# An attention scheduler that keeps two engines out of each other's way in its plan, and a new order

## The chip, the cores and the metric

One core of a Trainium2 chip runs the whole program. The time is in device microseconds for one execution. Engines: PE (matrix products), DVE, ACT and POOL (elementwise work), SP (issues most DMAs). Each engine takes its instructions from a queue of its own, in the order in which the program put them there; semaphores tie the queues together.

## The reference

Three layers in a row, in float32:

```python
q_rot, k_rot = rotate(q), rotate(k)              # 4 batches, 8 heads, 576 positions, 64 columns
attn = softmax(q_rot @ k_rot.T / sqrt(64))
x = (attn @ v).transpose(0, 2, 1, 3).reshape(2304, 512)
x = (sigmoid(x @ w_gate) * (x @ w_val)) @ w_out  # 512 -> 1536 -> 512
e = argmax(x @ w_gate2 + bias[modality])         # one of 8 experts for each token
out = prob[e] * (relu(x @ w1[e]) @ w2[e])        # 512 -> 1024 -> 512
```

## The kernel before

The three layers stand one behind the other: the attention (class `Attention`), the gated layer (`Gated`) and the experts (`Experts`). Products of float32 are made from two parts of a number, a high part (a cast) and a low part (the number less its high part), so nearly every tile gets a cast on ACT or POOL and a subtraction on DVE or POOL.

The attention works on 16 pairs of heads (p), each in 9 tiles of 128 query rows (T = 9 p + t). For a tile:

- PE makes the scores (`scores`, L183) into one of 2 PSUM tiles `s`;
- DVE takes them out, scaled, with the row minimum (`evac_scores`, L193), into one of 11 tiles `e`;
- ACT makes the exponentials with their sums (`exp`, L205);
- PE transposes them in four pieces (`transpose`, L237) into one of 3 PSUM tiles `pt`;
- ACT casts the high part `pth` (`pt_hi`, L267) and DVE subtracts for the low part `ptl` (`pt_lo`, L271).

When half a pair's tiles are there, PE multiplies by v (`value`, L284); ACT copies one half of the result (L292) and DVE adds (`value_add`, L301) into `xy`. Later the row sums, sent through DRAM as `rr`, normalise the pair's outputs (`normalise`, L231, on DVE or POOL).

The preparation of a pair runs one pair ahead. SP loads q and k with their half-swapped copies into `sa` (L328). For each half (q is 0, k is 1) POOL or DVE multiplies by the rotation table (`rope_op`, L162 for both products at once, 1152 columns; L164 for one) and adds (L160); then comes the cast (L152 on ACT, L154 on POOL) and the low part (L437: `sa<-sa` for q, `kl<-sa` for k, on DVE or POOL). SP then copies the parts to other partitions (L455). v gets a cast and a low part too (L349). The next load of a half waits until the low part of the same half is made. Pairs 0 and 1 go another way (`plan_direct`): the rotation is cut into pieces of columns (L164, L160), k-low is L383 and q-low L398. The conversion of the first gated weights (L654 to L681) fills gaps.

The order in every queue is made by `Plan` while the program is built. Each operation is added with its engine, an assumed cost, the operations it needs and a priority. `order` keeps a clock for each engine; it takes the engine that can start something first and, of what is ready there, the operation of the lowest priority number. An operation is done a latency `LAT` after its cost. Limits on buffers (`rings`) are counted too. Tables say who does what: `DIRECT` and `KLO` (pieces of pairs 0 and 1 on POOL), `LO`, `HI`, `VLO`, `VHI`, `ROPE`, `RM` (an engine for a pair's low part, cast, v, rotation, normalisation). `PR` and `OFF` move the priorities of kinds of operations against a tile's number.

The plan sets only the order in the queues. On the chip an instruction starts when its engine is free and its semaphores have come; the planned start times are not kept.

Below is what the change touches.

Of the kernel before, what the change touches and what calls it, by code (L numbers as in the profile page):

```python
# [31 lines left out]
class Plan:  # L32
# [4 lines left out]
    LAT = {"PE": 0.25, "SP": 0.65, "DMA": 2.0}  # L37

    def __init__(self, rings=(), free=()):
        self.ops = []  # L40
        self.free = dict(free)
        self.rings = dict(rings)
        self.takes = {}
        self.frees = {}

    def add(self, eng, cost, fn, deps, prio, ring=None):
# [5 lines left out]
    def order(self):  # L52
# [11 lines left out]

        def at(i):
            r = self.takes.get(i)
            if r and len(taken[r]) >= self.rings[r]:
                t = done[self.frees[taken[r][-self.rings[r]]]]
                return float("inf") if t is None else max(t, ready[i])
            return ready[i]  # L70
# [6 lines left out]
        while len(out) < n:  # L77
# [12 lines left out]
            free[e] = end  # L90
            self.start[i] = t
# [15 lines left out]
class Attention:  # L107
# [197 lines left out]
    def op(self, key, eng, cost, fn, deps=(), prio=0.0, ring=None):  # L305
# [5 lines left out]
        self.ids[key] = self.plan.add(eng, cost, fn, ds, prio, ring)  # L311
# [150 lines left out]
    DIRECT = ((0, 0, 0, 0), (0, 0, 1, 0), (0, 1, 0, 0), (0, 1, 0, 2), (1, 0, 0, 0), (1, 0, 0, 2), (1, 1, 0, 0), (1, 1, 0, 2),)  # L462
    NDIRECT = 2
    KLO = ((0, 0, 0), (0, 1, 1), (1, 0, 0),)
    LO = dict.fromkeys(((4, 0), (4, 1), (5, 0), (6, 0), (6, 1), (7, 1), (8, 0), (8, 1), (9, 1), (11, 1), (12, 0), (12, 1), (14, 1), (15, 0), (15, 1),), "POOL")
    VLO = dict.fromkeys((9, 14,), "DVE")
    ROPE = dict.fromkeys(((1, 0), (1, 1), (2, 0), (6, 0),), "DVE")
    PR = dict(ahead=-5.46, k=-139.78, split=-159.58, v=-65.53)
    RM = dict.fromkeys((0, 1, 2, 4, 5, 6, 7, 10, 12, 15,), "DVE")
    HI = dict.fromkeys(((2, 0), (2, 1), (3, 0), (5, 0), (6, 0), (6, 1), (7, 1), (8, 0), (9, 1), (10, 1), (11, 0), (12, 1), (13, 0), (14, 0), (14, 1), (15, 0),), "POOL")  # L470
    VHI = dict.fromkeys((1, 2, 4, 8, 9, 10,), "POOL")
    OFF = dict(table=0.16, xs=728.99, gv=822.87, post=977.12, rr=92.46, rm=165.62, s=-46.75, tsa=13.27, exp=86.93, eps=-141.16, rec=-185.35, norm=-135.21, tr=37.99, hi=46.49, lo=16.94, tr5=-62.52, val=70.55, vc=-103.28, va=-328.79)
# [138 lines left out]
class Gated:  # L611
# [202 lines left out]
    def opening(self):  # L814
# [10 lines left out]
        def op(key, eng, cost, fn, deps, prio, ring=None):  # L825
            ids[key] = plan.add(eng, cost, fn, [ids.get(d) for d in deps], prio, ring)
# [857 lines left out]
```

## Time and profile before

| | us |
|---|---|
| median of 3 runs | 1053.02 |
| lowest, highest run | 1049.65, 1053.76 |
| the profiled execution | 1049.16 |
| its span, first to last instruction | 1046.8 |
| PE busy in the span | 994.3 (95%) |
| DVE busy | 680.7 (65%) |
| ACT busy | 530.6 (51%) |
| POOL busy | 367.8 (35%) |

The shares of the whole span mix the three layers: the attention takes the first 320 us or so, the gated layer goes on to about 800 us, the experts take the rest. Which engine sets the pace has to be read for a stretch of time. Busy time is from start to end of an instruction as recorded, so an instruction that stands still half way counts as busy.

### The profile page before, as it was taken

Reading aid. Unit: us, or ns where it says so; the run is one execution under the profiler, and the core shown is the slowest. Engines: PE = TensorE matmul, PEld = TensorE weight load, DVE = VectorE, ACT = ScalarE, POOL = GpSimd, SP = SyncE. Lnnn points to the kernel's source line nnn. Section 1 sums busy time; section 2 is a strip of 40 time slices with the busy share of each in tenths; the row PEclk is TensorE's granted clock in tenths of the full one; section 3 lists DMA queues with packets and bytes.
Section 4 is the critical chain, followed back from the end, with each engine's and each line's share of the span. In section 5 each row is a group of like instructions: output and inputs, shape, how many; then the busy total and the mean of one; then the engine's idle time right before and its main releaser. Section 6 shows DMA issues by size and latency. Waiting matters only on the chain.

```text
span 1046.8 us, 16540 instructions
## 1 busy us (share of the span) xinstructions
PE 994.3 (95%) x6035; PEld 910.9 (87%) x6035; DVE 680.7 (65%) x1194; ACT 530.6 (51%) x1045; POOL 367.8 (35%) x279
## 2 busy tenths in 40 slices
PE   4989999989999999999999999999997999999996
PEld 2779898888998999999999999998975899999995
DVE  7999999999986756545535535522376755555651
ACT  5879898889886523212222212223331645555542
POOL 5578578677312422223223223311161012111111
PEclk9999999999999999999999999999998899999998
DMA  6568677767521311101101101000046877766650
GB/s 192 170 152 226 148 200 182 193 173 200 146 62 54 99 43 42 61 21 47 55 21 61 41 21 61 21 1 1 1 133 183 305 232 233 221 221 223 221 171 24
DMA packets 74136, 127.23 MB, mean 122 GB/s; under 512 B 14447, under 2 KB 37631, under 8 KB 74048
## 3 DMA queue, kind: packets, MB, share of 16 engines
q1 hardware_dynamic: 60128, 108.53, 35.7%
q0 software_dynamic: 3040, 9.70, 2.8%
q10 hardware_dynamic: 10880, 7.87, 2.4%
q8 instruction: 50, 0.82, 0.3%
q14 instruction: 38, 0.31, 0.1%
HBM read 95.65 MB, written 9.77 MB: 101 GB/s over the span
## 4 chain that ended last, share of the span: by engine, by line
PE 52%; issue 18%; DVE 16%; DMA 8%; POOL 3%; ACT 3%; SPq 0%; POOLq 0%; DVEq 0%; ACTq 0%
PE gv L721 28%; PE yo L787 13%; DMA out<-e_y,r_si 5%; DVE e L193 5%; DVE ptl L271 4%; PE pv L284 3%; PE s L183 3%; PE pt L237 2%; POOL e_xg L1452 1%; DVE xy L301 1%; ACT e L205 1%; PE s L721 1%; DMA sb<-sa 1%; PE r_pl L1221 1%; PE r_pt L1185 1%
## 5 line engine op out<-in xcount | busy, mean ns | idle before, releaser
L730 POOL TENSOR_TENSOR gl<-sg,gh 128x384 fp32r<-128x384 f32 x60 | 64.8, 1079 | 266.3 <-ACT gh L729 266.3
L728 DVE TENSOR_TENSOR sg<-gv,sg 128x384 f32<-128x384 f32 x70 | 39.0, 557 | 139.9 <-PE gv L721 119.9
L205 ACT ACTIVATE e<-e,st 128x576 f32<-128x576 f32 x144 | 112.3, 782 | 21.2 <-DVE e L193 20.5
L1445 DVE TENSOR_TENSOR e_w<-wr,e_w 128x1024 fp32r<-128x1024 f32 x80 | 96.0, 1223 | 28.4 <-ACT e_w L1444 28.1
L727 ACT ACTIVATE sg<-gv 128x384 f32<-128x384 f32 x70 | 34.4, 491 | 146.5 <-PE gv L721 146.3
L193 DVE TENSOR_SCALAR_CACHE_REDUCE e<-s 128x576 f32<-128x576 f32 x144 | 105.9, 744 | 1.6 <-PE s L183 0.9
L183 PE MATMUL s<-sb 128*128 128x288 f32 x320 | 78.8, 337 | 21.6 <-DVE sb L398 14.0
L271 DVE TENSOR_TENSOR ptl<-pt,pth 128x512 fp32r<-128x512 f32 x144 | 95.1, 679 | 1.5 <-ACT pth L267 0.4
L1444 ACT CAST e_w<-wr 128x1024 fp32r<-128x1024 f32 x80 | 81.5, 1048 | 23.1 <-DMA x_rows<-xy 20.6
L1500 PE MATMUL e_py<-e_w,e_hh 128*128 128x512 f32 x288 | 89.6, 392 | 0.0
L1515 POOL DMA_INDIRECT out<-e_y,r_si x19 | 19.6, 1030 | 187.7 <-ACT e_y L1514 177.5
L237 PE MATMUL pt<-cst,e 128*128 128x128 f32 x576 | 81.3, 279 | 3.0 <-DVE ptl L271 2.8
L267 ACT CAST pth<-pt 128x512 fp32r<-128x512 f32 x144 | 79.2, 587 | 7.7 <-PE pt L237 6.7
L1482 PE MATMUL e_ph<-e_xh,e_w 128*128 128x256 f32 x576 | 82.0, 286 | 0.7 <-ACT e_xh L1465 0.7
L162 POOL TENSOR_TENSOR sa<-sa,rope 128x1152 f32<-128x1152 f32 x26 | 69.5, 2674 | 37.1 <-DMA sa<-in_qk 29.6
L729 ACT CAST gh<-sg 128x384 fp32r<-128x384 f32 x60 | 30.8, 514 | 99.6 <-DVE sg L728 99.6
L183 PEld LDWEIGHTS s<-sb 128*128 128x128 f32 x320 | 51.3, 200 | 32.9 <-DVE sb L398 14.6
L284 PE MATMUL pv<-pth,vv 128*128 128x256 f32 (+1 forms) x256 | 73.9, 311 | 5.8 <-DVE xy L301 4.1
L721 PE MATMUL gv<-xe,wb 128*128 128x384 f32 x384 | 78.9, 338 | 0.0
L1482 PEld LDWEIGHTS e_ph<-e_xh,e_w 128*128 128x128 f32 x576 | 75.9, 195 | 1.7 <-ACT e_xh L1465 1.1
L721 PE MATMUL gv<-xh,wb 128*128 128x384 f32 x288 | 74.1, 338 | 0.0
L237 PEld LDWEIGHTS pt<-cst,e 128*128 128x128 f32 x576 | 67.9, 143 | 7.0 <-DVE ptl L271 2.8
(246 smaller groups left out, 2493.3 us busy)
## 6 DMA issues: line engine op xcount, KB each, us to landing
wr<-in_w SPq DMA_DIRECT2D x74, 512.0 KB
sa<-in_qk SPq DMA_DIRECT2D x30, 576.0 KB
sb<-sa SPq DMA_DIRECT2D x84, 144.0 KB
wraw<-in_wg SPq DMA_DIRECT2D x12, 512.0 KB
wraw<-in_wv SPq DMA_DIRECT2D x12, 512.0 KB
wraw<-in_wo SPq DMA_DIRECT2D x12, 512.0 KB
vraw<-in_v SPq DMA_DIRECT2D x16, 320.0 KB
x_rows<-xy ACTq DMA_DIRECT2D x18, 256.0 KB
```

The source lines that it names most:

```text
L183: nc.tensor.matmul(ps[:, u, 0:SH], a, m[:, SH * u:SH * u + SH], start=n == 0, stop=n == len(mm) - 1)
L193: self.nc.vector.tensor_scalar(out=e, in0=ps[:, :, 0:SH], scalar1=-0.125, scalar2=3.0e38, op0=ALU.mult, op1=ALU.min, accum_out=st[:, 0])
L205: nc.scalar.activation(out=e, in_=e, func=AF.Exp, bias=st[:, 0], scale=-1.0, accum_out=st[:, 1])
L237: nc.tensor.transpose(pt[:, c], e[:, 128 * c:128 * c + 128], self.ident)
L271: self.nc.vector.tensor_tensor(out=lo, in0=src, in1=f32(hi), op=ALU.subtract)
L284: nc.tensor.matmul(ps[:, 0:w], a, m, start=n == 0, stop=n == len(mm) - 1)
L721: self.nc.tensor.matmul(p[:, 0:U], a[:, wc], b[:, c], start=c == 0 and n == 0, stop=c == KC - 1 and n == 2)
L787: nc.tensor.matmul(ps, a, b, start=n == 0, stop=n == 3 * len(GROUPS[grp]) - 1)
L1444: nc.scalar.copy(out=hi, in_=raw)
L1445: nc.vector.tensor_tensor(out=lo, in0=raw, in1=f32(hi), op=ALU.subtract)
L1482: nc.tensor.matmul(ps[:, k], a[:, fs], b[:, c], start=n == 0, stop=n == 3 * KC - 1)
L1500: nc.tensor.matmul(ps, a[:, f, hs], b, start=n == 0, stop=n == 23)
```

## The change

The planner gets a set `shared`: all operations of POOL, and those of DVE that read two operands from SBUF or belong to the conversion of weights (normalisation, low parts of v, q and k, rotation, parts of x, the last step of the gate). It keeps one clock `port` for the set: a shared operation cannot start before the last shared one has ended, on whichever of the two engines that was. The assumed DMA latency goes from 2.0 to 2.2. All tables of shares and priorities get new numbers. No instruction is added to the program, and none gets another shape except the pieces of pairs 0 and 1 that change engine.

```diff
-    LAT = {"PE": 0.25, "SP": 0.65, "DMA": 2.0}
+    LAT = {"PE": 0.25, "SP": 0.65, "DMA": 2.2}
...
-    def add(self, eng, cost, fn, deps, prio, ring=None):
+        self.shared = set()
+
+    def add(self, eng, cost, fn, deps, prio, ring=None, shared=False):
+        if shared and eng == "DVE" or eng == "POOL":
+            self.shared.add(len(self.ops))
...
+        port = 0.0
+
         def at(i):
             r = self.takes.get(i)
+            t0 = max(ready[i], port) if i in self.shared else ready[i]
             if r and len(taken[r]) >= self.rings[r]:
                 t = done[self.frees[taken[r][-self.rings[r]]]]
-                return float("inf") if t is None else max(t, ready[i])
-            return ready[i]
+                return float("inf") if t is None else max(t, t0)
+            return t0
...
             free[e] = end
+            if i in self.shared:
+                port = end
...
-        self.ids[key] = self.plan.add(eng, cost, fn, ds, prio, ring)
+        shared = key[0] in ("rm", "vlo", "rope", "rot", "klo", "qlo", "xs", "cv") or key[0] == "lo" and len(key) == 3
+        self.ids[key] = self.plan.add(eng, cost, fn, ds, prio, ring, shared or key[0] == "post" and key[2] == 3)
...
-    KLO = ((0, 0, 0), (0, 1, 1), (1, 0, 0),)
+    KLO = ((0, 1, 1), (1, 0, 0), (1, 1, 0),)
...
-    PR = dict(ahead=-5.46, k=-139.78, split=-159.58, v=-65.53)
+    PR = dict(ahead=-305.08, k=-8.83, split=-1473.89, v=-316.64)
...
-            ids[key] = plan.add(eng, cost, fn, [ids.get(d) for d in deps], prio, ring)
+            ids[key] = plan.add(eng, cost, fn, [ids.get(d) for d in deps], prio, ring, key[0] in ("xl", "cv"))
```

What the other tables say, counted: low parts of q and k on POOL, 20 in place of 15 of 28 (both of a pair in nine pairs, in place of five); low parts of v on DVE, 6 in place of 2 of 16; normalisations on DVE, 7 in place of 10 of 16; casts of q and k on POOL, 13 in place of 16; casts of v on POOL, 7 in place of 6; pieces of the first two rotations on POOL, 5 in place of 8. The whole rotations (L162) on DVE stay two. In the changed file the lines stand 8 further down, from the middle of the class on 9.

Two places of the order. First POOL at the start, around the k-low of pair 1 (`kl_100`). Before:

```order
L164 TENSOR_TENSOR sa<-sa,rope 128x576
L383 TENSOR_TENSOR kl_100<-sa,sb 64x576
L160 TENSOR_TENSOR sa<-sa 128x576
L154 TENSOR_SCALAR vv_98<-vraw 128x10x64
L681 TENSOR_TENSOR wr<-wt,wr 128x512
L349 TENSOR_TENSOR vv_98<-vraw,vv_98 128x10x64
L162 TENSOR_TENSOR sa<-sa,rope 128x1152
```

and with the change:

```order
L172 TENSOR_TENSOR sa<-sa,rope 128x576
L168 TENSOR_TENSOR sa<-sa 128x576
L690 TENSOR_TENSOR wr<-wt,wr 128x512
L392 TENSOR_TENSOR kl_100<-sa,sb 64x576 x2
L170 TENSOR_TENSOR sa<-sa,rope 128x1152
L168 TENSOR_TENSOR sa<-sa 128x576
```

The addition for q that stood behind the k-low and both operations on v have left this piece of POOL's queue; the second k-low, which was DVE's, has come in, right ahead of the first whole rotation of pair 2.

Second DVE in pair 5 (numbers tell tiles apart: an `e` is a tile's scores as evacuated, a `pt` its transposed exponentials). Before, from the evacuation of `e_1430` to its low part, which is `pt_1515`:

```order
L193 TENSOR_SCALAR e_1430,st_1331<-s_1377 128x576
L271 TENSOR_TENSOR ptl_94<-pt_1399,pth_93 128x4x128
L193 TENSOR_SCALAR e_1447,st_1331<-s_1408 128x576
L193 TENSOR_SCALAR e_1457,st_1331<-s_1441 128x576
L301 TENSOR_TENSOR xy_73<-pv_1415,xv_105 64x256
L271 TENSOR_TENSOR ptl_94<-pt_1433,pth_93 128x4x128
...
L193 TENSOR_SCALAR e_1535,st_1331<-s_1503 128x576
L271 TENSOR_TENSOR ptl_94<-pt_1515,pth_93 128x4x128
```

and with the change, from `e_1403` to its low part, which is `pt_1435`:

```order
L201 TENSOR_SCALAR e_1403,st_1404<-s_1388 128x576
L201 TENSOR_SCALAR e_1418,st_1404<-s_1396 128x576
L446 TENSOR_TENSOR kl_0_99<-sa_103 128x576
L446 TENSOR_TENSOR sa_103<-sa_103 128x576
L309 TENSOR_TENSOR xy_73<-pv_1406,xv_105 64x320
L279 TENSOR_TENSOR ptl_94<-pt_1435,pth_93 128x4x128
L279 TENSOR_TENSOR ptl_94<-pt_1443,pth_93 128x4x128
```

Before, the low part stands 13 rows behind the evacuation (the fence leaves out six), which is the median of all 144 tiles; with the change five rows, where the median is 9. The preparation's low parts now stand ahead of the exponentials' when both can be had.

## Rows read from the trace of the kernel before

**Rows 1.** Busy time by stretch (us), instructions; PE, PEld, DVE, ACT, POOL; clock, DMA.

```profile
110.00:140.00 30.00, 28.32 (x221) 27.15 (x220) 29.67 (x68) 26.53 (x64) 23.20 (x14) 1.00 0.75 187
230.00:260.00 30.00, 28.83 (x223) 27.55 (x222) 28.86 (x65) 27.35 (x65) 22.17 (x15) 1.00 0.68 180
420.00:500.00 80.00, 80.00 (x426) 75.30 (x425) 38.94 (x58) 19.91 (x38) 21.55 (x19) 1.00 0.15 47
```

**Rows 2.** Groups of DVE, 0 to 322 us: busy us, mean ns, idle us before.

```profile
L193 DVE TENSOR_SCALAR_CACHE_REDUCE e<-s 128x576 f32<-128x576 f32 x144 | 105.9, 744 | 1.6 <-PE s L183 0.9
...
L231 DVE TENSOR_TENSOR xy<-xy,rr 128x576 f32<-128x576 f32 x10 | 13.2, 1317 | 1.6 <-DMA rr<-recip_rows 1.5
...
L437 DVE TENSOR_TENSOR sa<-sa 128x576 fp32r<-128x576 f32 x8 | 8.7, 1088 | 0.0
...
L383 DVE TENSOR_TENSOR kl<-sa,sb 64x576 fp32r<-64x576 f32 x1 | 4.7, 4685 | 0.0
L663 DVE TENSOR_SCALAR wt<-wt 128x512 int32<-128x512 int32 x3 | 4.6, 1544 | 0.0
...
L672 DVE SCALAR_TENSOR_TENSOR wt<-wraw,wt 128x512 int32<-128x512 int32 x3 | 3.5, 1180 | 0.0
...
L658 DVE TENSOR_SCALAR wt<-wt 128x512 f32<-128x512 f32 x3 | 3.1, 1037 | 0.0
```

**Rows 3.** Single lines on DVE: ns shortest/median/longest, first and last start, forms.

```profile
L437 DVE TENSOR_TENSOR sa<-sa x8: 736/1046/1593, 47.0 to 252.4; 128x576 fp32r<-128x576 f32 x8
...
L663 DVE TENSOR_SCALAR wt<-wt x36: 411/427/2675, 19.2 to 669.7; 128x512 int32<-128x512 int32 x36
...
L672 DVE SCALAR_TENSOR_TENSOR wt<-wraw,wt x36: 681/692/1668, 21.6 to 675.5; 128x512 int32<-128x512 int32 x36
...
L271 DVE TENSOR_TENSOR ptl<-pt,pth x144: 623/681/693, 25.0 to 310.2; 128x512 fp32r<-128x512 f32 x144
...
L164 DVE TENSOR_TENSOR sa<-sa,rope x7: 446/529/1757, 5.6 to 23.7; 128x288 f32<-128x288 f32 x3, 128x576 f32<-128x576 f32 x2, 128x256 f32<-128x256 f32 x1, 128x320 f32<-128x320 f32 x1
```

**Rows 4.** Timeline from 26 us: start us, us, engine, line; POOL without a break.

```profile
26.26 1.40 POOL L160 TENSOR_TENSOR sa<-sa 128x576 f32<-128x576 f32 x1
...
27.02 4.68 DVE L383 TENSOR_TENSOR kl<-sa,sb 64x576 fp32r<-64x576 f32 x1
...
29.55 1.53 POOL L349 TENSOR_TENSOR vv<-vraw,vv 128x640 fp32r<-128x640 f32 x1
```

**Rows 5.** Timeline around 209 us: DVE beside POOL.

```profile
208.79 2.67 POOL L162 TENSOR_TENSOR sa<-sa,rope 128x1152 f32<-128x1152 f32 x1 [1.59 <-DMA sa<-in_qk]
...
208.99 3.09 DVE L231 TENSOR_TENSOR xy<-xy,rr 128x576 f32<-128x576 f32 x1
```

**Rows 6.** Groups of POOL, 0 to 322 us.

```profile
L162 POOL TENSOR_TENSOR sa<-sa,rope 128x1152 f32<-128x1152 f32 x26 | 69.5, 2674 | 37.1 <-DMA sa<-in_qk 29.6 <-DVE rt L218 2.4 <-DVE e L193 2.0
L160 POOL TENSOR_TENSOR sa<-sa 128x576 f32<-128x576 f32 x28 | 42.4, 1522 | 3.1 <-DVE sa L164 2.3
...
L437 POOL TENSOR_TENSOR kl<-sa 128x576 fp32r<-128x576 f32 x9 | 14.1, 1561 | 10.4 <-PE s L183 10.2
...
L231 POOL TENSOR_TENSOR xy<-xy,rr 128x576 f32<-128x576 f32 x6 | 8.6, 1431 | 24.6 <-DMA rr<-recip_rows 12.8 <-DVE ptl L271 6.9 <-DVE xy L301 4.8
```

**Rows 7.** Waits, 0 to 322 us: us in total, times, longest us.

```profile
POOL sa L162 <- DMA sa<-in_qk: 29.6, 15, 5.3
```

**Rows 8.** Groups of ACT, 0 to 322 us.

```profile
L205 ACT ACTIVATE e<-e,st 128x576 f32<-128x576 f32 x144 | 112.3, 782 | 21.2 <-DVE e L193 20.5
L267 ACT CAST pth<-pt 128x512 fp32r<-128x512 f32 x144 | 79.2, 587 | 7.7 <-PE pt L237 6.7
```

**Rows 9.** Timeline of DVE: the first evacuation of pair 1, and of pair 15.

```profile
37.66 0.75 DVE L193 TENSOR_SCALAR_CACHE_REDUCE e<-s 128x576 f32<-128x576 f32 x1
...
285.81 0.74 DVE L193 TENSOR_SCALAR_CACHE_REDUCE e<-s 128x576 f32<-128x576 f32 x1
```

More of the change, by code (lines that the diff above doesn't have):

```diff
@@ L460, in plan_prep @@
         self.ready[p] = [[("dup", p, 0), ("dup", p, 1), ("lo", p, 1)]] * TPP
-    DIRECT = ((0, 0, 0, 0), (0, 0, 1, 0), (0, 1, 0, 0), (0, 1, 0, 2), (1, 0, 0, 0), (1, 0, 0, 2), (1, 1, 0, 0), (1, 1, 0, 2),)
+    DIRECT = ((0, 0, 0, 1), (0, 0, 0, 2), (0, 0, 1, 2), (1, 0, 0, 0), (1, 1, 0, 2),)
     NDIRECT = 2
-    KLO = ((0, 0, 0), (0, 1, 1), (1, 0, 0),)
-    LO = dict.fromkeys(((4, 0), (4, 1), (5, 0), (6, 0), (6, 1), (7, 1), (8, 0), (8, 1), (9, 1), (11, 1), (12, 0), (12, 1), (14, 1), (15, 0), (15, 1),), "POOL")
-    VLO = dict.fromkeys((9, 14,), "DVE")
-    ROPE = dict.fromkeys(((1, 0), (1, 1), (2, 0), (6, 0),), "DVE")
-    PR = dict(ahead=-5.46, k=-139.78, split=-159.58, v=-65.53)
[L469 to L472, printed above, removed]
+    KLO = ((0, 1, 1), (1, 0, 0), (1, 1, 0),)
+    LO = dict.fromkeys(((2, 1), (3, 0), (3, 1), (4, 1), (5, 0), (5, 1), (7, 0), (7, 1), (9, 0), (9, 1), (11, 0), (11, 1), (12, 0), (12, 1), (13, 0), (13, 1), (14, 0), (14, 1), (15, 0), (15, 1),), "POOL")
+    VLO = dict.fromkeys((0, 1, 3, 4, 6, 11,), "DVE")
+    ROPE = dict.fromkeys(((3, 0), (7, 0),), "DVE")
+    PR = dict(ahead=-305.08, k=-8.83, split=-1473.89, v=-316.64)
+    RM = dict.fromkeys((0, 1, 2, 8, 12, 14, 15,), "DVE")
+    HI = dict.fromkeys(((2, 0), (2, 1), (4, 0), (5, 0), (5, 1), (6, 0), (7, 0), (8, 1), (9, 1), (12, 0), (12, 1), (14, 0), (14, 1),), "POOL")
+    VHI = dict.fromkeys((0, 2, 6, 10, 12, 13, 15,), "POOL")
+    OFF = dict(table=-290.25, xs=530.11, gv=1162.52, post=861.37, rr=492.73, rm=742.08, s=12.20, tsa=342.45, exp=518.13, eps=61.87, rec=-555.16, norm=-583.85, tr=44.38, hi=230.96, lo=-149.60, tr5=-348.65, val=195.71, vc=96.93, va=-440.32)
     def plan_tile(self, T):
```

## Prediction

> **What bounds the kernel now.** I read the busy table by stretch first. From about 330 us to the end the program is TensorE's: the stretch 420 to 500 has PE busy 80.00 of 80 us [rows 1]. The change moves nothing that PE does there, so what the attention (0 to 320 us) wins or loses arrives whole at the end. Inside the attention the fullest engine is DVE: 29.67 of 30 us and 28.86 of 30, against 28.32 and 28.83 for PE, 26.53 and 27.35 for ACT, 23.20 and 22.17 for POOL [rows 1]. A shorter DVE queue is a shorter attention, until PE is next: it has 1.68 and 1.17 us per 30 free, some 1.4.
>
> Then the groups of DVE by line and form. Two kinds cost the same every time: the evacuation of the scores (744 ns, 144 of them) and the low part of the transposed exponentials (L271: 623 to 693 ns over 144) [rows 2, 3]. Each reads PSUM. The operations that read only SBUF vary: the low part of q on DVE goes from 736 to 1593 ns, the 512-wide clamp and shift of a weight's conversion from 411 to 2675, the bitwise step from 681 to 1668 [rows 3].
>
> Two places say why. At 208.79 POOL begins a rotation product of 2.67 us; at 208.99 DVE begins a normalisation that alone takes 0.74. It ends at 212.08, 0.62 after POOL's operation [rows 5]. At 27.02 DVE's k-low waits through a whole run of POOL, from the operation begun at 26.26 to the one ending at 31.08, and ends at 31.70 [rows 4]. So DVE's SBUF operations stand still while POOL works, and every later score and exponential in DVE's queue stands behind them.
>
> What that costs, group by group, mean less the undisturbed time [rows 2, 3]: normalisation 10 x (1.317 - 0.736) = 5.8 us; q-low 8 x (1.088 - 0.736) = 2.8; k-low 4.685 - 0.736 = 3.9; the shifts 3 x (1.544 - 0.411) = 3.4; the bitwise or 3 x (1.180 - 0.681) = 1.5; the clamps 3 x (1.037 - 0.411) = 1.9; the longest rotation product of the start 1.757 - 0.446 (the shortest of its line) = 1.3. The sum is 20.6 us: 5.2 at the start (k-low and the product), 15.4 later. It is an upper bound of what the exclusion can give.
>
> **The change, part by part.** (1) *Start.* The second k-low of pair 1 joins the first on POOL, and DVE gets back what is on balance one rotation piece and a half-width k-low of pair 0 and two pieces of pair 1. The stall of 3.9 us goes, and the product of 1.757 us meets one POOL product at most, not two. In exchange k-low costs POOL twice DVE's time, in front of pair 2's first rotation, and SP's queue holds pair 2's loads behind it. As these loads waited for the stalled k-low too, they should not come later. Bounds 0 and 5.2; I take 4, nearer the upper, because the longest stall is removed by the move itself and not by timing.
>
> (2) *Shares.* DVE loses five lows of q or k and three normalisations (8 x 0.736 = 5.9 us) and gets four lows of v (640 columns, worked out from 0.736 at 576: 0.82 each, 3.3) and the pieces of part 1 less its k-low (1184 columns on balance, 1.5 at the same rate). Together about 1.0 us less. POOL gets the mirror: 5 x 1.56 + 3 x 1.43 more, 4 x 1.53 and the pieces less [rows 4, 6], near zero in sum. ACT takes three casts of POOL and gives one: it has 3 us of 30 free [rows 1].
>
> (3) *The exclusion.* The planner now starts a shared DVE operation only when its own clock has POOL idle, and the other way. It adds no wait to the program: on the chip POOL begins its next operation as soon as its data are there. It holds as far as planned and real times agree within a POOL operation (1.4 to 2.7 us [rows 6]); but a rotation begins when a load lands, and POOL waited for those 15 times, 29.6 us in all, up to 5.3 [rows 7], so the phases drift. Bounds: 15.4 us gained, and 0 (below nothing too, if phases fall worse). I take half, 7.7, since the operations that follow their own POOL producer keep their place while those after a load do not.
>
> (4) *Order.* The priorities now drain: the exponentials' low parts and value adds come first, new scores last but one. Of a tile, the median distance on DVE between evacuating its scores and its low part falls from 13 rows to 9, the shortest from 8 to 5. Between them lie the exponential on ACT (782 ns), four transposes, and the cast on ACT (587 ns) [rows 8]; with the evacuation 0.744 + 0.782 + 0.587 = 2.1 us before the transposes count. Five rows, as in the second order excerpt, last 2 x 0.744 + 2 x 0.736 = 3.0 us and a value add. That is nearly no slack, where before there was slack for every tile. No wait of this kind is in the trace to be priced: its low end is 0, its high end one in four of 144 tiles waiting for one cast, 36 x 0.587 = 21 us. I take 3.5, nearer the low end, because ACT is not full. The new DMA latency and the marks on later plans change order alone, under a PE that never stops: nothing.
>
> Sum: 4 + 1.0 + 7.7 - 3.5 = 9.2 us, say 9. The profiled execution took 1049.2 us (span 1046.8 and 2.4 around it), so it would be 1040; the median of the runs is 1053.0, 3.9 higher, and gives **1044**.
>
> At part 1 a rule disagrees with the trace. DVE's k-low was held through a run of POOL operations [rows 4]. The Trainium skill, "SBUF — State Buffer", section "Summary: rules for kernel authors", says that the second to issue is blocked until the first finishes. By it the wait would have ended at 27.66, and part 1 would be worth under 2 us; the trace shows 31.08.
>
> **The rivals.** *A: the order does not hold.* The exclusion lives in the planner only. If real phases are as random as before, part 3 is worth nothing, and 4 + 1.0 - 3.5 = 1.5 remains: 1051.5, no change. For it: no wait is added. Against it: DVE's shared operations are fewer after the start, and the planner knows of the conflict. The Trainium skill, same page, section "Who interferes with whom", says that issue order decides who blocks, and the first one holds the shared port pair for its whole instruction; by that rule a plan that is right but for a fifth of a microsecond still loses a whole POOL operation, and the time is this rival's. The trace agrees on who waits: POOL was ahead by 0.20 us [rows 5].
>
> *B: POOL's preparation becomes the bound, slower.* Nine of the later pairs have both lows on POOL, against five. Such a pair needs 2 x 2.67 + 2 x 1.52 + 2 x 1.56 + 1.53 + 1.43 = 14.5 us of POOL [rows 4, 6], and the pairs pass every (285.81 - 37.66) / 14 = 17.7 us [rows 9]. It decides once POOL waits over 3.2 us a pair for loads. With two mean waits (2 x 29.6 / 15 = 3.9 [rows 7]) a pair takes 18.4, nine of them 6 us more, and what DVE saves is lost behind it: 1059. Against: POOL's sum stays.
>
> *C: the short distance bites, slower.* If one tile in four waits for one cast, 21 in place of 3.5 comes off: 12.7 - 21, or 1061. It decides from 22 waiting tiles on (12.7 / 0.587). Against: ACT has spare time.
>
> *D: the exclusion holds entirely.* Then PE caps it: 1.4 us per 30 over 248 us is 11.6 after the start, and with 5.2 there 17: 1036. PE's busy time is modelled, so that cap is soft; without it 21.6, or 1031.
>
> **How the numbers follow.** Forecast 0.50, A 0.23, B 0.08, C 0.07, D 0.12. About 0.5% (5.3 us) is what a measurement here can tell from no change. Faster: D and the forecast but for 0.04 of it, 0.58. Same: A and that 0.04, 0.27. Slower: B and C, 0.15. The range goes from 1031 (D without its cap) to 1057, just short of B and C; it leaves out those and little else.
>
> **What would show it.** Right: in the changed profile the means of DVE's normalisation and q-low come to 0.9 us or less; no DVE operation lasts over 3 us at the start; pair 1's first evacuation comes before 35 us and pair 15's before 278; PE stays full from 330 us less the gain. A would show as means unchanged on other operations; B as more idle time of POOL's rotation behind the loads, with scores waiting for the copies that follow; C as idle time of DVE before L279, ended by ACT's cast, of over 10 us. The forecast is wrong if DVE's busy share in the attention stays at 29.7 of 30 with the same length.

## The result, and the profile after

The change makes the kernel slower: 1062.8 us (median of 4 runs, 1059.4 to 1064.9) against 1051.6 (4 runs), a ratio of 1.0103 with the interval 1.0066 to 1.0140. The forecast was 1044, the range 1031 to 1057. The profiled execution took 1063.9 us, its span is 1062.1; the trace of before has 1046.8. These two executions lie 14.7 us apart, the medians 11.2, since the one profiled before took less than any of the four timed; the stretches, waits and pairs below are from the traces.

First the busy time by stretch of the change, columns as in [rows 1]: PE, PEld, DVE, ACT, POOL; clock, DMA.

```profile
0.00:335.00 335.00, 290.04 (x2043) 266.15 (x2044) 288.99 (x640) 263.49 (x611) 194.26 (x126) 0.97 0.60 158
...
110.00:140.00 30.00, 26.27 (x198) 24.23 (x197) 27.42 (x61) 24.81 (x59) 16.75 (x11) 1.00 0.72 198
...
230.00:260.00 30.00, 26.17 (x191) 23.64 (x189) 23.33 (x53) 21.85 (x52) 22.82 (x16) 0.99 0.65 160
...
420.00:500.00 80.00, 80.00 (x422) 74.80 (x421) 40.98 (x66) 21.09 (x43) 22.62 (x20) 1.00 0.15 47
```

And of before, the attention alone:

```profile
0.00:319.10 319.10, 286.70 (x2045) 264.72 (x2046) 300.45 (x641) 262.56 (x609) 195.59 (x127) 0.99 0.64 169
```

PE is full from 420 to 500 us in both, and from the last value add of the attention to the end the two traces take 727.7 and 727.1 us. So the loss lies in the attention. Its last value add ends at 319.1 us before and at 335.0 after:

```profile
318.64 0.49 DVE L301 TENSOR_TENSOR xy<-pv,xv 64x320 f32<-64x320 f32 x1
```

```profile
334.48 0.49 DVE L309 TENSOR_TENSOR xy<-pv,xv 64x320 f32<-64x320 f32 x1 [0.66 <-ACT xv L300]
```

These 15.9 us explain the 15.3 by which the spans differ. Up to that point DVE is busy for 288.99 us in place of 300.45, so **11.5 us of its work are gone**, as the change meant. But it is idle for 335.0 - 289.0 = 46.0 us in place of 319.1 - 300.45 = 18.65: **27.4 us of new waiting**. 27.4 - 11.5 = 15.9. DVE was all but full in the two stretches of [rows 1]; now it has 2.6 and 6.7 us of 30 free, and PE and ACT do less in the same stretch too.

The groups of DVE up to 338 us, answering to [rows 2] (busy us, mean ns, idle before):

```profile
L201 DVE TENSOR_SCALAR_CACHE_REDUCE e<-s 128x576 f32<-128x576 f32 x144 | 105.4, 747 | 9.2 <-PE s L191 8.5
L279 DVE TENSOR_TENSOR ptl<-pt,pth 128x512 fp32r<-128x512 f32 x144 | 93.1, 682 | 6.6 <-ACT pth L275 5.6
...
L358 DVE TENSOR_TENSOR vv<-vraw,vv 128x640 fp32r<-128x640 f32 x6 | 8.0, 1337 | 0.1
...
L239 DVE TENSOR_TENSOR xy<-xy,rr 128x576 f32<-128x576 f32 x7 | 6.4, 921 | 1.6 <-DMA rr<-recip_rows 1.5
L446 DVE TENSOR_TENSOR sa<-sa 128x576 fp32r<-128x576 f32 x5 | 3.7, 749 | 0.0
...
L672 DVE TENSOR_SCALAR wt<-wt 128x512 int32<-128x512 int32 x3 | 1.8, 597 | 0.0
```

DVE's operations on SBUF are shorter. The normalisation's mean falls from 1317 to 921 ns, q-low's from 1088 to 749, the shift's from 1544 to 597 [rows 2]. The low part of v is still stretched (1337 where it takes 808 in excl_only, below). I add up, over all DVE operations up to the last value add, what each takes beyond the shortest of its form in these two traces, where that is over 0.1 us: 23.8 us in 25 operations before, 9.8 in 14 after. I call this sum **the stretch** below.

What the change costs is in the waits of DVE, from 15 us on (us in total, times, longest). Of before:

```profile
DVE xy L301 <- ACT xv L292: 3.8, 2, 2.5
...
DVE e L193 <- PE s L183: 0.9, 2, 0.8
...
DVE ptl L271 <- ACT pth L267: 0.4, 1, 0.4
```

Of the change:

```profile
DVE xy L309 <- ACT xv L300: 13.4, 18, 2.8
DVE e L201 <- PE s L191: 8.5, 11, 1.8
DVE ptl L279 <- ACT pth L275: 5.6, 14, 0.7
DVE p5l L279 <- ACT p5h L275: 5.0, 4, 2.9
```

Value adds wait for ACT's copy 9.6 us longer than before, low parts (`ptl`, and `p5l`, which had no such wait) for ACT's cast 10.2, evacuations for scores 7.6. Together they are 27.4 us, the size of the new idle time; the smaller waits cancel.

POOL's wait for loads, answering to [rows 7], has grown too:

```profile
POOL sa L170 <- DMA sa<-in_qk: 47.7, 17, 6.5
```

With it, the chain of work that ended last (page of the profile, shares of the span by engine) is made of other things. Before, DVE has 16% of it, DMA 8% and SP's queue 0%; in the change:

```profile
PE 50%; issue 17%; DMA 13%; DVE 9%; ACT 4%; POOL 3%; SPq 3%; POOLq 0%; DVEq 0%; ACTq 0%
```

Loads of q and k make 4.9% of that chain, 52 us in seven pieces of up to 8.7. In the chain of before a single load stands, 6.97 us.

The pairs, answering to [rows 9]: the first evacuations of pairs 1, 2 and 15 in the change.

```profile
37.03 0.75 DVE L201 TENSOR_SCALAR_CACHE_REDUCE e<-s 128x576 f32<-128x576 f32 x1
...
69.34 0.76 DVE L201 TENSOR_SCALAR_CACHE_REDUCE e<-s 128x576 f32<-128x576 f32 x1
...
307.45 0.69 DVE L201 TENSOR_SCALAR_CACHE_REDUCE e<-s 128x576 f32<-128x576 f32 x1
```

Before, pair 2 begins at 60.18. Pair 1 is 0.6 us earlier, pair 2 is 9.2 later, pair 15 is 21.6 later. (The last pair then ends 5.7 us sooner after its start: in the change 7 value adds and 11 tiles' low parts are still to come when it begins, before 9 and 15.)

The widest gap is between pairs 1 and 2: 19 us from the start of the last evacuation of one to the start of the first of the other, 6 us before. The timeline there, with the idle time before an instruction in brackets:

```profile
55.36 0.55 PE L292 MATMUL pv<-pth,vv 128*128 128x256 f32 x1 [3.28 <-DVE xy L309]
...
57.87 0.37 ACT L300 COPY xv<-pv 64x256 f32<-64x256 f32 x1 [3.81 <-PE pv L292]
...
60.57 0.55 PE L292 MATMUL pv<-pth,vv 128*128 128x256 f32 x1 [0.40 <-DVE xy L309]
...
62.75 0.43 DVE L309 TENSOR_TENSOR xy<-pv,xv 64x256 f32<-64x256 f32 x1 [1.23 <-ACT xv L300]
...
63.23 0.41 PE L292 MATMUL pv<-pth,vv 128*128 128x320 f32 x1 [0.96 <-DVE xy L309]
...
66.03 0.41 PE L292 MATMUL pv<-pth,vv 128*128 128x320 f32 x1 [1.07 <-DVE xy L309]
...
67.60 0.43 PE L191 MATMUL s<-sb 128*128 128x288 f32 x2
```

The four value products of pair 1 stand in PE's queue one behind the other, ahead of the first scores of pair 2. They share one PSUM tile (the plan's ring `pv` is 1), so each waits until ACT has copied and DVE has added the product before it, 2.7 to 5.2 us a round, and PE, ACT and DVE wait for each other in turn. The longer rounds are not ACT's alone: of the product ahead of these four, ACT's copy is done at 52.37 us and DVE's add begins at 54.72, behind the conversion of a weight, one clamp of it stretched to 1.75 us. Before, pair 2's scores stand between pair 1's value products (the last piece of two products, and scores):

```profile
57.82 0.28 PE L284 MATMUL pv<-p5l,vv 128*128 128x256 f32 x1
...
58.30 0.51 PE L183 MATMUL s<-sb 128*128 128x288 f32 x2
...
64.76 0.28 PE L284 MATMUL pv<-p5l,vv 128*128 128x256 f32 x1
```

Counted over the whole attention up to the last evacuation: two value adds with no evacuation between them occur 2 times before, 14 times in the change.

### The profile page after: what moved, and what is told of

It reads as the page before. It is cut to its first block, busy times and chain, and to the rows that moved or that the text cites. A ratio compares the mean times of both kernels' runs of the same rounds, so it can differ in the third digit from the quotient of the medians.

```text
span 1062.1 us, 16574 instructions
## 1 busy us (share of the span) xinstructions
PE 995.4 (94%) x6035; PEld 910.6 (86%) x6035; DVE 669.2 (63%) x1193; ACT 531.9 (50%) x1047; POOL 365.9 (34%) x278
## 4 chain that ended last, share of the span: by engine, by line
PE 50%; issue 17%; DMA 13%; DVE 9%; ACT 4%; POOL 3%; SPq 3%; POOLq 0%; DVEq 0%; ACTq 0%
PE gv L730 28%; PE yo L796 13%; DMA out<-e_y,r_si 5%; DMA sa<-in_qk 5%; PE pv L292 3%; DVE e L201 2%; SPq L464 2%; PE s L191 2%; DVE ptl L279 2%; POOL e_xg L1461 1%; ACT e L213 1%; DMA rr<-recip_rows 1%; PE pt L245 1%; PE s L730 1%; PE r_pl L1230 1%
## 5 line engine op out<-in xcount | busy, mean ns | idle before, releaser
L279 DVE TENSOR_TENSOR ptl<-pt,pth 128x512 fp32r<-128x512 f32 x144 | 93.1, 682 | 6.6 <-ACT pth L275 5.6
L245 PE MATMUL pt<-cst,e 128*128 128x128 f32 x576 | 84.0, 280 | 5.7 <-ACT e L213 3.9
L170 POOL TENSOR_TENSOR sa<-sa,rope 128x1152 f32<-128x1152 f32 x26 | 69.6, 2676 | 53.2 <-DMA sa<-in_qk 47.7
L191 PEld LDWEIGHTS s<-sb 128*128 128x128 f32 x320 | 50.4, 196 | 36.7 <-DVE sb L407 12.9
L245 PEld LDWEIGHTS pt<-cst,e 128*128 128x128 f32 x576 | 67.9, 144 | 12.2 <-ACT e L213 8.8
```

The source lines that it names most:

```text
L191: nc.tensor.matmul(ps[:, u, 0:SH], a, m[:, SH * u:SH * u + SH], start=n == 0, stop=n == len(mm) - 1)
L245: nc.tensor.transpose(pt[:, c], e[:, 128 * c:128 * c + 128], self.ident)
L279: self.nc.vector.tensor_tensor(out=lo, in0=src, in1=f32(hi), op=ALU.subtract)
```

## The experiments

Eighteen kernels. The theories: **exclusion** (rival A or the forecast: does the plan's exclusion hold on the chip), **distance** (the mechanism of rival C: operations are queued too close behind what they wait for; where an expectation says theory D, it is this one, not the prediction's rival D), **late loads** (rival B's sign; theory P in the expectations), and **tables** (T: the numbers of before were found for one order, and any other order loses).

| kernel | us | ratio to before, 95% | stretch | DVE idle | distance | plan's end |
|---|---|---|---|---|---|---|
| the kernel before | 1051.6 | | 23.8 | 15.6 | 13 | 282.2 |
| the change | 1062.8 | 1.0103 [1.0066, 1.0140] | 9.8 | 43.3 | 9 | 312.5 |
| excl_only | 1066.8 | 1.0171 [1.0125, 1.0217] | 10.5 | 35.7 | 9 | 310.6 |
| no_excl | 1066.9 | 1.0162 [1.0124, 1.0200] | 19.1 | 36.7 | 16 | 303.2 |
| old_shares | 1066.3 | 1.0143 [1.0103, 1.0183] | 14.0 | 40.7 | 9 | 312.2 |
| old_pr | 1069.1 | 1.0173 [1.0133, 1.0213] | 12.2 | 47.6 | 9 | 309.3 |
| lat_only | 1055.6 | 1.0062 [1.0039, 1.0086] | 18.7 | 25.0 | 13 | 292.4 |
| cost_only | 1054.2 | 1.0053 [1.0029, 1.0078] | 21.6 | 22.2 | 12 | 288.1 |
| before_pad | 1054.0 | 1.0051 [1.0029, 1.0073] | 14.8 | 32.9 | 16 | 302.9 |
| before_small | 1046.8 | 0.9981 [0.9965, 0.9998] | 20.6 | 17.3 | 13 | 282.2 |
| after_small | 1055.0 | 1.0050 [1.0020, 1.0079] | 9.6 | 32.9 | 9 | 312.5 |
| after_pad | 1051.9 | 1.0004 [0.9984, 1.0024] | 15.3 | 31.0 | 14 | 312.2 |
| after_dma | 1086.8 | 1.0346 [1.0323, 1.0370] | 16.8 | 55.9 | 8 | 345.5 |
| after_pad_dma | 1066.3 | 1.0154 [1.0131, 1.0177] | 14.1 | 39.2 | 10 | 342.5 |
| pad_act | 1059.8 | 1.0088 [1.0048, 1.0128] | 14.5 | 37.5 | 10 | 312.6 |
| pad_pe | 1064.2 | 1.0123 [1.0092, 1.0155] | 8.9 | 44.8 | 12 | 319.3 |
| pad_no_excl | 1062.4 | 1.0094 [1.0060, 1.0129] | 17.1 | 40.7 | 14 | 312.9 |
| pad_half | 1058.8 | 1.0090 [1.0058, 1.0122] | 10.6 | 38.1 | 12.5 | 314.1 |
| pad_big | 1066.5 | 1.0146 [1.0113, 1.0179] | 15.3 | 42.9 | 20 | 336.1 |
| pad_small | 1048.6 | 0.9969 [0.9950, 0.9988] | 16.4 | 25.5 | 14 | 312.2 |

Stretch and idle time (us, of DVE, from 5.6 us, its first rotation product, to the last value add) are summed from one trace of each; the idle time is some 3 us less than in the section before, where the first 5.6 us count too. The ratio is to the kernel before in the same batch. Distance is the median over 144 tiles of the rows on DVE between evacuating a tile's scores and its low part; the plan's end is where the planner's own clock has the last value add of the attention. Both are read off the program as it is built, not off the chip. A longer assumed latency can lengthen the plan's clock by itself, so its ends compare best between plans with the same latencies.

### The exclusion alone, and everything but the exclusion

excl_only is the new scheduler with the tables and latencies of before; against the change:

```diff
-    LAT = {"PE": 0.25, "SP": 0.65, "DMA": 2.2}
+    LAT = {"PE": 0.25, "SP": 0.65, "DMA": 2.0}
...
-    KLO = ((0, 1, 1), (1, 0, 0), (1, 1, 0),)
+    KLO = ((0, 0, 0), (0, 1, 1), (1, 0, 0),)
```

(and so for every table). no_excl is the change with the port's clock standing still:

```diff
-            if i in self.shared:
-                port = end
```

> The scheduler of the change with the tables and the DMA latency of before. Theory P (the new order lets the preparation of a pair come just in time, so that the scores wait for its copies): the tables are to blame, not the exclusion, so this is 1040 to 1053 us, copies end 4 us or more before a pair's first evacuation. Rival X (the exclusion itself, by holding POOL back in the plan, delays the preparation): 1058 to 1066 us, POOL waiting 40 us or more for loads.

> All tables and the latency of the change, but the planner's port clock never advances, so nothing is excluded. P: still slow, 1058 to 1070 us, DVE's stretched time back at 20 us. X: 1048 to 1054 us.

With the tables of before, the exclusion takes the stretch from 23.8 to 10.5 us; with those of the change, from 19.1 (no_excl) to 9.8. Three groups of DVE in excl_only, then the same three in no_excl:

```profile
L239 DVE TENSOR_TENSOR xy<-xy,rr 128x576 f32<-128x576 f32 x9 | 7.4, 818 | 0.0
...
L446 DVE TENSOR_TENSOR sa<-sa 128x576 fp32r<-128x576 f32 x8 | 6.2, 769 | 0.0
...
L358 DVE TENSOR_TENSOR vv<-vraw,vv 128x640 fp32r<-128x640 f32 x2 | 1.6, 808 | 0.0
```

```profile
L237 DVE TENSOR_TENSOR xy<-xy,rr 128x576 f32<-128x576 f32 x7 | 8.5, 1221 | 0.1
...
L444 DVE TENSOR_TENSOR sa<-sa 128x576 fp32r<-128x576 f32 x5 | 7.3, 1470 | 0.3 <-ACT sa L158 0.3
...
L356 DVE TENSOR_TENSOR vv<-vraw,vv 128x640 fp32r<-128x640 f32 x6 | 6.3, 1044 | 0.1
```

Each is to be held against the kernel with the same tables. Excl_only against before: normalisation 818 for 1317 ns, q-low 769 for 1088. The change against no_excl: normalisation 921 for 1221, q-low 749 for 1470, but v's low part 1337 for 1044, so not every group gains. By these two pairs of plans, one trace each, the plan's exclusion reaches the chip and rival A falls; a third pair further down says that it need not do so in every plan.

And yet excl_only is 1.7% slower than before, with 20 us more of idle time on DVE. The order that comes out has the short distances (median 9 rows, shortest 5) even with the old priorities, and value adds with no evacuation between them 13 times. The tables without the exclusion lose as much (1.0162), though their median distance, 16 rows, is longer than before's 13: short distances are not what they lose by, or not alone. Each half of the change by itself costs at least what both cost together. So neither theory of these two runs holds as stated: P had excl_only at 1040 to 1053 us, X had no_excl at 1048 to 1054.

### One table at a time

old_shares is the change with the eight tables of shares of before; old_pr is the change with `PR` of before:

```diff
-    PR = dict(ahead=-305.08, k=-8.83, split=-1473.89, v=-316.64)
+    PR = dict(ahead=-5.46, k=-139.78, split=-159.58, v=-65.53)
```

> The change with the eight tables of shares (DIRECT, KLO, LO, VLO, ROPE, RM, HI, VHI) of before, priorities new. P: priorities are to blame, 1056 to 1068 us. Rival S (more low parts on POOL lengthen the preparation): 1046 to 1054 us.

> The change with the four numbers PR of before alone (priorities of the preparation against the tiles). P in its narrow form (preparation ranked too late): 1044 to 1054 us and 4 us or more between the copies and a pair's first evacuation. If the tiles' own order (OFF) or the shares are to blame: 1058 to 1068 us.

1.0143 and 1.0173, neither below the change's 1.0103: neither the shares nor `PR`, put back, give the loss back. old_pr was expected at 1044 to 1054 if the preparation is ranked too late, and that reading falls. `OFF`, the tiles' own priorities, was not put back alone.

### Small changes to the plan of before

lat_only takes DMA's latency alone, cost_only alters the assumed cost of an evacuation by 10 ns, both on the kernel before:

```diff
-    LAT = {"PE": 0.25, "SP": 0.65, "DMA": 2.0}
+    LAT = {"PE": 0.25, "SP": 0.65, "DMA": 2.2}
```

```diff
-        self.op(("tsa", T), "DVE", 0.665, lambda: self.evac_scores(T), [("s", T)], T + o["tsa"], "e")
+        self.op(("tsa", T), "DVE", 0.675, lambda: self.evac_scores(T), [("s", T)], T + o["tsa"], "e")
```

> The kernel before with the assumed DMA latency 2.2 for 2.0 and nothing else. Theory T (the tables of before are fitted to one order, and any new order, whatever its reason, gives some 1% away): 1058 to 1068 us, DVE idle 30 us or more in the attention. Theory E (it is the exclusion or the new tables that lose, a small change of the plan does not): 1048 to 1055 us.

> The kernel before with the assumed cost of evacuating a tile's scores 0.675 for 0.665 us and nothing else. T: 1058 to 1068 us with 30 us or more of idle DVE. E: 1048 to 1055 us.

Both lose half a per cent (1.0062, 1.0053), with 7 to 9 us more idle time of DVE, though no engine got more work. Neither edit says anything about the chip. The theory of the tables (T) had expected 1058 to 1068 and 30 us of idle time, so as stated it fails; half of its loss is there, at the upper end of what theory E had expected. What stays is that a new order can lose some 5 us against that of before, whatever it is meant to do. That does not carry the whole 11 us, and these two runs do not tell it from "distance".

### Small loads, order untouched

after_small and before_small keep every instruction in its place and leave out most of the loads of q and k from pair 3 on: 16 of 576 columns come, the rest is what lay there.

```diff
-            return lambda: nc.sync.dma_start(out=self.raw[:, h, cols], in_=self.qk[b, hp, :, h, cols])
+            c = slice(0, 16) if p > 2 else cols
+            return lambda: nc.sync.dma_start(out=self.raw[:, h, c], in_=self.qk[b, hp, :, h, c])
```

> The change with its order untouched; the loads of q and k of pairs 3 to 15 bring 16 of 576 columns, so they land early (the rest is what lay there). P (the preparation, behind its loads, sets the pace of the pairs): 1045 to 1054 us, idle DVE down by 10 us or more. If the waits are on the tiles' own chain (scores, exponential, cast, value and its copy): 1059 to 1064 us.

> The same on the kernel before. P: the copies there stand 6 us ahead of the first evacuation, so nothing is to be won: 1046 to 1053 us. If loads bound both kernels: 1035 to 1045 us.

The change gets back 1.0103 - 1.0050 = 0.53%, 5.6 us, by the two intervals give or take as much again; before gains 0.19%, 2.0 us. The time, 1055.0, falls between the two ranges expected. POOL's wait for loads falls from 47.7 to 13.4 us, but DVE still waits:

```profile
DVE xy L309 <- ACT xv L300: 10.1, 17, 2.2
DVE e L201 <- PE s L191: 6.7, 10, 1.6
DVE ptl L279 <- ACT pth L275: 5.0, 13, 0.7
```

Late loads are a part of the loss, 3.6 to 5.6 of 11 us, by putting pairs later (pair 15 begins at 296.5 in place of 307.4). The rest stays without them; the other steps of the preparation (POOL's work, SP's copies) are as they were in this run, so it does not clear those.

### More slack in the plan, and more distrust of the loads

after_pad raises what the planner assumes between the end of an operation on PE or ACT (which had the default, 0.13) and its use elsewhere, and changes nothing else; before_pad does it to the kernel before; after_dma raises DMA's latency instead, after_pad_dma both:

```diff
-    LAT = {"PE": 0.25, "SP": 0.65, "DMA": 2.2}
+    LAT = {"PE": 0.55, "ACT": 0.45, "SP": 0.65, "DMA": 2.2}
```

```diff
-    LAT = {"PE": 0.25, "SP": 0.65, "DMA": 2.2}
+    LAT = {"PE": 0.25, "SP": 0.65, "DMA": 5.0}
```

> The change with longer assumed latencies behind PE (0.55 for 0.25 us) and ACT (0.45 for 0.13), so that the plan puts a consumer later: the median distance from evacuation to low part goes from 9 rows back to 14. Theory D (no slack in the order: each small difference between plan and chip makes DVE wait for ACT): DVE's waits for ACT (value add, low parts; 27 us in the change) fall under 15 us, and the time to 1050 to 1058 us. If only the loads matter: waits move, 1060 to 1066 us.

> The same latencies on the kernel before, whose distance was 13 rows and becomes 16. D: no gain, as there was slack; T gives the 5 us of any new order: 1051 to 1058 us. Stretched time of DVE stays at 18 us or more.

> The change with an assumed DMA latency of 5.0 us, about what its loads took. P: the plan now knows how late loads land and asks for the preparation in time; the copies stand 5 us or more ahead of a pair's first evacuation, 1052 to 1060 us. If the loads come as early as they can already: 1060 to 1068 us.

> Both together. D and P each with its share: 1046 to 1054 us, idle DVE under 25 us with stretched time under 13. If the order before is simply a fitted one (T): not under 1053 us.

before_pad loses what the small changes lost (1.0051), as both theories had it; its stretch, expected at 18 us or more, falls to 14.8 with no exclusion at all, so a mere new order moves the stretch as well. after_pad, in the range that theory D expected, stands level with the kernel before (1.0004): two assumed numbers give back the whole loss. The median distance is 14 rows again, and unseparated value adds come 7 times in place of 14. One of its stretches and DVE's waits:

```profile
230.00:260.00 30.00, 28.86 (x222) 27.54 (x221) 28.31 (x65) 26.90 (x64) 24.43 (x15) 1.00 0.78 204
```

```profile
DVE xy L309 <- ACT xv L300: 9.0, 13, 2.3
DVE e L201 <- PE s L191: 6.3, 11, 2.1
DVE ptl L279 <- ACT pth L275: 5.7, 12, 1.2
```

PE has 222 instructions between 230 and 260 us, as before (223 [rows 1]), where the change has 191. The value adds wait 4.4 us less than in the change, the scores 2.2; the wait of `p5l` (5.0) is gone from the list. The tiles' low parts (`ptl`) wait as long as in the change (5.7 us, 5.6), although their median distance went from 9 rows to 14. POOL still waits 45.9 us for loads, so it isn't they that came sooner.

Believing loads to be slower made it much worse (1.0346, outside both ranges expected), and spoiled after_pad too (1.0154, where 1046 to 1054 us was expected if both theories have their share). The order of after_dma has distances of 8 rows in the median and 5 at the shortest, and DVE's idle time grows to 55.9 us.

### Which slack, and how much

Four kernels split the two latencies, take half the step, and take the exclusion out of after_pad:

```diff
-    LAT = {"PE": 0.25, "SP": 0.65, "DMA": 2.2}
+    LAT = {"PE": 0.25, "ACT": 0.45, "SP": 0.65, "DMA": 2.2}
```

```diff
-    LAT = {"PE": 0.25, "SP": 0.65, "DMA": 2.2}
+    LAT = {"PE": 0.55, "SP": 0.65, "DMA": 2.2}
```

```diff
-    LAT = {"PE": 0.25, "SP": 0.65, "DMA": 2.2}
+    LAT = {"PE": 0.40, "ACT": 0.29, "SP": 0.65, "DMA": 2.2}
```

```diff
-    LAT = {"PE": 0.25, "SP": 0.65, "DMA": 2.2}
+    LAT = {"PE": 0.55, "ACT": 0.45, "SP": 0.65, "DMA": 2.2}
...
-            if i in self.shared:
-                port = end
```

> The change with ACT's assumed latency alone raised, 0.45 for 0.13. Both latencies together gave back 11 us (1051.9). If the lost slack is that behind ACT's casts and copies, as the waits of the change say (value add behind ACT's copy 13.4 us, low part behind its cast 10.6), this one alone gives most of it: 1052 to 1056. If it is the scores on PE that are too tight, or if any other order would have done as well, it stays at 1060 to 1064.

> The change with PE's assumed latency alone raised, 0.55 for 0.25. If the slack behind ACT's casts is what was missing, this moves little: 1059 to 1063. If it was the slack between PE's scores and their evacuation (8.5 us of DVE's waits), it gives the larger part: 1052 to 1056.

> The change with both latencies raised half as far (PE 0.40, ACT 0.29). If the time follows the slack smoothly, it lies between 1062.8 and 1051.9, near 1057. If each plan is a throw of its own, it can lie anywhere from 1050 to 1067, and a step of one latency tells little by itself.

> The change with both latencies raised (1051.9) and without the exclusion (the port's clock never moves). If the exclusion is worth what it removes of the stretching of DVE once the order has slack, this is slower by about half of the 9 us between the stretching with it and without it: 1056 to 1061. If the exclusion only tightens the order and slack was all that mattered, it is as fast or faster: 1046 to 1052, and would be the first to beat the kernel before.

ACT's latency alone gives back little if anything (1.0088), PE's nothing (1.0123): neither expectation of "most of it" held. Nor do the waits follow the latencies: with ACT's raised the low parts wait 10.3 us for its cast, not 5.6, and with PE's raised the value adds wait 17.5 us for ACT's copy, not 13.4. Half of both gives 1.0090 (1058.8, not far from the 1057 expected), the whole 1.0004. pad_no_excl is 0.9% slower than after_pad, a little above the range expected if the exclusion is worth something, so with these latencies the plan with it is the better one. But its stretch (17.1) is hardly above after_pad's (15.3): in this third pair of plans the exclusion keeps next to nothing away. What differs is the idle time, 40.7 against 31.0. The difference is again one of order, and can't be booked as the exclusion's gain.

The last two take a larger step, and small loads in after_pad (as the edit above):

```diff
-    LAT = {"PE": 0.25, "SP": 0.65, "DMA": 2.2}
+    LAT = {"PE": 0.75, "ACT": 0.65, "SP": 0.65, "DMA": 2.2}
```

> The change with both latencies raised further (PE 0.75, ACT 0.65). Half the step gave 1058.8, the whole step 1051.9, against 1062.8 without. If the missing slack still sets the time, a larger step gives a few us more, 1045 to 1050, and beats the kernel before. If the whole step had used up what slack can give, or if rings of buffers now stop the plan from running ahead, it is 1052 to 1058.

> The change with both latencies raised as in the run of 1051.9, its order untouched, and the loads of q and k of pairs 3 to 15 only 16 of 576 columns (a part of the computation is thereby altered). POOL still waits 45.9 us for loads in that run, as against 47.7 in the change. If the order with slack still pays for the late loads, this gives back 5 us or more: 1047 or less. If the slack covers them, it gives back no more than the 2 or 3 us that small loads gave the kernel before: 1049 to 1052.

pad_big loses all of it again (1.0146, above both ranges expected). The low parts do wait less, but the evacuations wait in a way that the change did not know, for transposes:

```profile
DVE xy L309 <- ACT xv L300: 12.1, 14, 2.5
DVE e L201 <- PE pt L245: 7.8, 6, 1.7
DVE e L201 <- PE s L191: 7.2, 11, 1.5
...
DVE ptl L279 <- ACT pth L275: 2.5, 6, 1.3
```

An evacuation writes an `e` tile, and the transposes are what read it last. With more distance more tiles are under way; the row fits the 11 tiles `e` running out. That is 7.8 us of the 42.9 in which DVE is idle; the rest of the loss is not explained. pad_small gives 0.9969, 0.35% below after_pad: there the loads cost 3.7 us, between the two expectations and not far above the 2.0 that they cost the kernel before.

No version with full loads beat the kernel before; after_pad is level with it.

## Why the prediction was wrong

**The gains came about as forecast.** Parts 1, 2 and 3 were 4 + 1.0 + 7.7 = 12.7 us off DVE's work; its busy time fell by 11.5. Counted at the shortest time of each form, the work fell by 1.4 us (part 2 has 1.0). The stretch fell from 7.5 to 3.4 us up to 37.7 us, where pair 1 began (part 1 has 4), and from 16.4 to 6.5 later (part 3 has 7.7). Against this, 2.4 us come back because instructions that follow one another at once overlap in the records, by some 80 ns, and where DVE waits they do not: 38.6 us of overlap before, 36.2 after. The 20.6 us that the prediction called an upper bound were too few, as 23.8 were there.

That half of part 3's bound was near the mark was luck: the same rule took 13.3, 9.3 and 1.8 us off the stretch in three pairs of plans. Of the signs, q-low (749 ns) and the start (no DVE operation over 2.1 us) came as written, the normalisation (921 ns) just missed 0.9 us, and the pairs did not come: pair 1 at 37.0 in place of 35, pair 15 at 307.4 in place of 278.

By the rule of the Trainium skill that was cited for rival A ("SBUF — State Buffer", section "Who interferes with whom": issue order decides who blocks), a plan that is right but for a little would lose whole operations again and again. In two of the three pairs of plans the runs don't bear out that consequence, since about half of the stretch went (23.8 to 10.5, 19.1 to 9.8). In the third it hardly fell (17.1 to 15.3), and a collision that remains still costs up to 1.3 us, as at the clamp that took 1.75.

**The step that failed is part 4, the order, priced at 3.5 us.** DVE waited 27.4 us more. Four faults lie in that term. First, I priced one wait only, the low part behind ACT's cast, and took a value near its low end "because ACT is not full". A queue that runs in order does not wait for a full engine, it waits for one late operation: ACT has more free time after the change than before, and DVE waits for it 20 us more. The wait that I priced rose by 5.2 us (`ptl`), inside the bounds of 0 to 21; the same wait of `p5l`, which the 144 tiles leave out, brought 5.0 more. Second, the larger wait was not in the term at all: 9.6 us of value adds behind ACT's copy. The excerpt of the order that I read was DVE's; on PE's the value products had been drawn together, and with one `pv` tile each round costs a product, a copy and an add in series. Third, the evacuations' 7.6 us behind scores that come late. Fourth, the new DMA latency was put at nothing, "under a PE that never stops"; that holds behind the attention, but in it PE stops, and lat_only, with this number alone, loses 0.6%. One line on the order misled as well: the preparation's low parts did not come to stand ahead of the exponentials' with the change. Their priority numbers were lower before too, by some 160 and more.

**The planner's own clock was not read.** By that clock the attention ends at 282.2 us before and at 312.5 with the change, 30.3 later; the chip showed 15.9. Of the 30.3, the DMA latency alone has 10.2 (lat_only, 292.4). At that latency the new tables without the exclusion have 10.8 more (no_excl, 303.2), and with it 20.1. So the new tables do not win back what the exclusion adds to the plan, and the forecast of a faster attention stood against a plan that by its own count was slower.

**Part 1's "they should not come later" failed as well.** Pair 2 begins 9.2 us late. Its loads are issued 1.7 us later than before, POOL makes both of its rotations before the first low part, and PE's queue holds the scores behind the four value products of pair 1. From pair 2 on, rival B's sign stands in the profile as written: POOL's wait for loads rose from 29.6 to 47.7 us and PE's scores wait for copies (4.5 us in 6 waits, before 0.2):

```profile
PE s L191 <- DMA sb<-sa: 4.5, 6, 1.9
```

B had a chance of 0.08 and gave 1059, C 0.07 and 1061. The signs of both are there (C's, over 10 us of idle time behind ACT's cast before L279, by little: 10.6), and the time, 1062.8, is near both by luck. B's reason is not borne out: with the old shares, five pairs with both low parts on POOL in place of nine, the kernel is no faster (1.0143). C's reason was one wait in four tiles of 0.587 us; there were 14 such waits of 144, and the value adds cost more. That short distances and a late preparation come from the same order, and so were not two separate mishaps, is my reading; no run separates them.

**What is shown, and what isn't.** Shown: the loss is waiting of DVE in the attention; loads carry 3.6 to 5.6 us of it; another order of the same instructions, by two assumed latencies, gives the whole loss back. Shown in two pairs of plans of three: the exclusion shortens DVE's operations on the chip. Not shown: which property of the order costs the time. It isn't the median distance alone, as no_excl (16 rows), pad_big (20) and pad_pe (12) lose 1.2 to 1.6%, nor slack alone: after_pad's neighbours lie from 1.0088 to 1.0146, and edits of no meaning cost the old plan 0.5%. Plans scatter by some 5 us from one number to the next, and the change's, at 1.0103, lies within the scatter of its own neighbours. Nor is it settled which of the two waits behind ACT weighs more, since each step of a latency moves both.

## What to carry to other kernels

An order made by a planner is priced by the waits it makes, not only by the work it takes away: read in every queue, not just the fullest engine's, how far each operation stands behind what it waits for, and whether operations that share a single buffer have been drawn together. Neither settles the time by itself, as the runs show; read the planner's own end time as well, before and after: a plan that its own clock calls slower needs a reason to be faster on the chip. A freer engine is no cover for a short distance in an in-order queue. And before a planner's rule is judged by one plan, change a number that means nothing and see how far the time moves; here that was 0.5%, half the effect in question.

## What the runs showed of the hardware

Of two loads of q and k issued a microsecond apart, the second took longer than a load alone. Before, a load issued at 43.60 us, with copies behind it, let POOL's rotation begin at 48.57, 5 us later. In the change two loads go out together, with copies behind them (SP's queue), and POOL's second rotation waits:

```profile
202.19 0.33 SPq L337 DMA_DIRECT2D sa<-in_qk  x1
...
203.20 0.53 SPq L337 DMA_DIRECT2D sa<-in_qk  x1
...
211.39 2.66 POOL L170 TENSOR_TENSOR sa<-sa,rope 128x1152 f32<-128x1152 f32 x1 [1.08 <-DMA sa<-in_qk]
```

The second lands some 8 us after its issue. The kernel before has such a pair too, issued at 199.68 and 200.95: the rotations that waited for them begin at 204.52 and 208.79 [rows 5], 4.8 and 7.8 us later. Whether the other load or the copies hold the second up was not separated.

TensorE's clock also gave way in the gap between pairs 1 and 2. The same stretch of 6 us, before and in the change:

```profile
54.20:60.20 6.00, 4.51 (x38) 4.09 (x35) 5.94 (x12) 4.38 (x11) 6.00 (x5) 1.00 0.67 164
```

```profile
54.20:60.20 6.00, 4.82 (x21) 4.26 (x21) 3.92 (x9) 0.80 (x2) 4.78 (x3) 0.51 0.99 246
```

PE had stood idle for 3.28 us at 55.36, and the granted clock of the stretch is 0.51, that is the lower level, 1.2 GHz, for nearly all of it; 21 products are busy for longer than 38 were. Over the whole attention the clock falls from 0.99 to 0.97, and PE is busy 3.3 us longer for the same products (290.04 against 286.70). In the gap ten value products of 256 columns come 0.21 us apart, and 0.12 apart when the clock is back, at 61.5 us, so the clock accounts for a part; the rest was not taken apart.
